# An attention, expert and gated block on one core: the gate row by transposes, output stores issued two units late, the second weights loaded into borrowed tiles

## The chip, the core and the metric

The kernel runs on one core of a Trainium2 chip. The metric is the time of one execution on the device in microseconds, the median of several. A core has TensorE (matmuls; PE in the profile, PEld for its weight loads), VectorE (DVE), ScalarE (ACT), GpSimd (POOL) and SyncE (SP), whose queue here issues nearly all transfers between HBM and the on-chip memory SBUF. Matmuls write into the eight banks of PSUM, from which VectorE or ScalarE must read them before a bank is used again. Each engine works through its own list in order; semaphores order the engines among one another.

## The reference

Three steps follow each other: attention over 32 memory slots a head, a mixture of experts with one expert for each token, and a gated feed-forward layer. Cut to what matters here:

```python
a = softmax(phi); k_m = einsum('bhsm,bhsd->bhmd', a, k); v_m = einsum('bhsm,bhsd->bhmd', a, v)
x = softmax(q @ k_m.T / 8) @ v_m                  # 8 batches, 8 heads, 576 positions, 64 wide
logits = x @ w_gate + modality_bias[modality_id]  # 4608 tokens, 8 experts
e_idx = argmax(logits); gate_w = softmax(logits)[e_idx]
out[mask_e] = gate_w * (relu(x @ w1[e]) @ w2[e])  # 512 -> 1024 -> 512
out = (sigmoid(out @ w_gate2) * (out @ w_val)) @ w_out   # 512 -> 1536 -> 512
```

The code for experts other than the first stands behind a test at run time and is not entered in the profiled execution.

## The kernel before

All matmuls with 288 or more columns run in three terms: each float32 operand is cut into a high and a low part (`split`: a ScalarE cast, then a VectorE subtraction), and high times high, high times low and low times high are added in PSUM (`gemm`, L383 to L385).

**Prologue** (to about 45 us). Batch 0 gets its phi softmax, transposes, pooled keys and values (`pool_kv`, `keep_kv`), scores and the first weights folded with the pooled values (`fold`, which needs all of `w1s`). The second expert weights `w2` come in four parts of 512 KB, first as they are into a tile `late`, then split into `w2h` and `w2l`. `late` has the tag `kv`: it uses the same memory as the keys and values of batch 0. `warm` issues matmuls whose results nobody reads.

**Expert stage** (45 to about 530 us), one pass for each batch of 576 tokens. An `Expert` has 32 units: for each half of 288 tokens eight `hidden` units (six matmuls, evicted by ScalarE into `hh`, then by VectorE into `hl`) and eight half-tiles `y_part` (twelve matmuls; the second of a pair ends with VectorE's product of the PSUM tile and the gate row `gb`, L413, and the store of `yt` to the DRAM tensor `x2d`, L420). `side(i)` puts the preparation of later batches beside the units, at numbered slots: `scores`, `normalize`, `attn_transpose`, `gate_logits` and `gating` of the next batch, `phi_softmax`, `phi_transpose`, `pool_kv`, `keep_kv` and `gate_cols` (L248) of the one after, and two `fold` steps at slots 28 and 30, each of whose two PSUM banks are evicted by `split` (L116, L117). PSUM is shared out by tags: four banks `mm`, two `tr`, one `sc`, one `kv`.

**The gate row.** `gating` leaves a gate weight for each token in `gt`, 128 partitions by 5 columns. The expert needs it along the free axis on every partition. `gate_store` (L353) writes `gt` to a DRAM row `gd` in pieces of 4 bytes, `gate_rows` (L357) loads that row into all partitions as `gb`. Both stand on SyncE's queue, and the load waits until the store has landed.

**Rounding.** `Narrow` takes the weights of the third step, which come as 8-byte numbers, to float32: `load` brings 512 KB into one of two buffers `raw` (L437), `round` begins with a ScalarE step (L444), goes on with five on VectorE and one on GpSimd into one of two buffers `f`, and ends with a store to the DRAM tensor `wd` (L451). There are 36 of them, spread over the slots of the batches.

**Order.** The prologue keeps its written order (`in_order`). Elsewhere a scheduler orders each engine's list, so that roundings, for instance, end before batch 5.

**Gated stage** (from about 535 us). It reads `x2d` and `wd` in five blocks of tokens; its `Quad` and `Out` functions are the same before and after.

Of the kernel before, what the change touches and what calls it, by code (L numbers as in the profile page):

```python
# [18 lines left out]
P = 128  # L19
B, H, S, DH, M = 8, 8, 576, 64, 32  # L20
D = 512
# [20 lines left out]
def attn_moe_glu_kernel(ctx: ExitStack, tc: tile.TileContext, qT, phiT, kvp, mod, wg, mbias, w1, w2, wgv, out):  # L42
# [6 lines left out]

    x2d = dram.tile([P, NP, N], F32, name="x2d")  # L50
    wd = dram.tile([NC2, P, F2], F32, name="wd")
    gd = [dram.tile([1, NT * P], F32, name=f"gd{i}") for i in range(2)]
    sd = dram.tile([NC2, P, 4, 256], F32, name="sd")

    def ps_one(tag):
# [95 lines left out]
    class Att:  # L151
# [197 lines left out]
        def gating(self, bias=None, sel=None):  # L349
            run(self.gating_steps(bias, sel))  # L350

        def gate_store(self):
            nc.sync.dma_start(gd[self.odd].rearrange("o (t p) -> (o p) t", p=P), self.gt)  # L353

        def gate_rows(self):
            self.gb = ap.tile([P, S], F32, name="gb", bufs=2)
            nc.sync.dma_start(self.gb, gd[self.odd][:, :S].to_broadcast([P, S]))  # L357

    def fold(x, n, tags=("mm", "mm"), later=False):
        if x.first is not None and n == 0:  # L360
# [18 lines left out]
    def gemm(pm, steps, lo, hi):  # L379
        n = len(steps)  # L380
        for i in range(lo, hi):
# [2 lines left out]
            T.matmul(pm, wh, xl, start=False, stop=False)  # L384
            T.matmul(pm, wl, xh, start=False, stop=i == n - 1)  # L385

    class Expert:
        def __init__(self, a, add=False):
            self.a = a
# [2 lines left out]
        def hidden(self, half, fc):  # L392
            a = self.a
            if fc == 0:
                self.hh = ap.tile([P, F1 // P, HS], F32R, name="hh")
                self.hl = ap.tile([P, F1 // P, HS], F32R, name="hl")
            pm = ps_one("mm")[:, :HS]
            f = slice(fc * P, (fc + 1) * P)
            s = slice(half * HS, (half + 1) * HS)
            gemm(pm, [(a.vmh[:, g, f], a.vml[:, g, f], a.ahT[:, g, s], a.alT[:, g, s]) for g in range(2)], 0, 2)  # L400
            A.activation(self.hh[:, fc, :], pm, AF.Relu)  # L401
            V.scalar_tensor_tensor(out=self.hl[:, fc, :], in0=pm, scalar=0.0, in1=self.hh[:, fc, :].bitcast(F32), op0=ALU.max, op1=ALU.subtract)  # L402

        def y_part(self, half, dc, part):
            if part == 0:
                self.pm = ps_one("mm")[:, :HS]
            pm = self.pm
            d = slice(dc * P, (dc + 1) * P)
            steps = [(w2h[:, fc, d], w2l[:, fc, d], self.hh[:, fc, :], self.hl[:, fc, :]) for fc in range(F1 // P)]
            gemm(pm, steps, 4 * part, 4 * part + 4)  # L410
            if part == 1:
                yt = ap.tile([P, HS], F32, name="yt", bufs=2)
                V.tensor_tensor(out=yt, in0=pm, in1=self.a.gb[:, half * HS : (half + 1) * HS], op=ALU.mult)  # L413
                c0 = self.a.at_b * S + half * HS
                dst = x2d[:, dc, ds(c0, HS)]
                if self.add:
                    old = ap.tile([P, HS], F32, name="yold", tag="gt_old")
                    nc.sync.dma_start(old, dst)
                    V.tensor_tensor(out=yt, in0=yt, in1=old, op=ALU.add)
                nc.sync.dma_start(dst, yt)  # L420

        def units(self):
            u = []
# [5 lines left out]
    class Narrow:  # L429
# [9 lines left out]
        def round(self):  # L439
            top = self.raw[:, :, 1]  # L440
            nxt = self.raw.bitcast(U16)[:, :, 1]
            f = ap.tile([P, D], F32, name="f", bufs=2)
            fi, tf = f.bitcast(I32), self.raw.bitcast(F32)[:, :, 1]
            A.activation(f, tf, AF.Abs, scale=2.0**16)  # L444
            V.tensor_scalar(f, f, 2.0, None, op0=ALU.max)
            V.tensor_scalar(top, top, -0x80000000, None, op0=ALU.bitwise_and)
            V.scalar_tensor_tensor(out=fi, in0=fi, scalar=3, in1=top, op0=ALU.logical_shift_left, op1=ALU.bitwise_or)
            V.tensor_scalar(top, fi, -0x800000, None, op0=ALU.bitwise_and)
            V.scalar_tensor_tensor(out=tf, in0=nxt, scalar=2.0**-36, in1=tf, op0=ALU.mult, op1=ALU.mult)
            G.tensor_tensor(out=f, in0=f, in1=tf, op=ALU.add)  # L450
            nc.sync.dma_start(wd[self.c, :, self.lo : self.lo + D], f)  # L451

    routed = {}

# [11 lines left out]
    def other_experts(vm):  # L466
# [6 lines left out]
        with tc.For_i(1, E, 1) as e:  # L473
# [3 lines left out]
            with tc.If(mine > 0):  # L477
# [7 lines left out]
                with tc.For_i(0, B // 2, 1) as pair:  # L485
                    two = [Att(b, pair) for b in range(2)]
                    for a in two:
                        a.load_phi()
                        a.load_kv()
                        a.phi_softmax()  # L490
                        pool_batch(a)
                        a.vmh, a.vml = vm[a.b]
                    for a in two:
                        for n in range(2):
                            fold(a, n)
                    for a in two:
                        a.load_q()
                        for t in (0, 2, 4):
                            a.scores(t)
                            a.normalize(t)  # L500
                            a.attn_transpose(t)
                            a.gate_logits(t)
                        bias = ap.tile([P, NT, E], F32, name="bias1")
                        nc.sync.dma_start(bias, biasd[:, ds(a.at_b * NT, NT), :])
                        a.gating(bias, sel)
                        a.gate_store()
                        a.gate_rows()
                        run(Expert(a, add=True).units())

# [4 lines left out]
    def side(i):  # L514
        u = {}

        def at(slot, f, *args):
            u.setdefault(slot, []).append((f, *args))
# [16 lines left out]
        if i + 1 < B:  # L535
# [21 lines left out]
            at(15 + lag, c.attn_transpose, 4)  # L557
            at(16 + lag, c.gate_logits, 4)
            at(16 + lag, c.gating)
            at(21 if i else 28, c.gate_store)  # L560
            at(26 if i else 31, c.gate_rows)
            for n in range(2):
                at(28 + 2 * n, fold, c, n)
        if i + 2 < B:
# [1 line left out]
        if i == 0:  # L566
            at(0, b0.gate_logits, 0)
            at(1, b0.gate_logits, 2)
            at(1, b0.attn_transpose, 4)
            at(2, b0.gate_logits, 4)  # L570
            at(2, w2_parts[3].split)
            at(4, b0.gating)
            at(6, b0.gate_store)
            at(8, b0.gate_rows)
            at(6, bat[2].load_kv)
            at(8, in_order, start)
        lo = max(0, 5 * i - 2)
        for k, n in enumerate(range(lo, min(5 * i + 3, NK))):
            w = Narrow(n)
            slot = 6 * k if i else 11 + 6 * k  # L580
            at(slot, w.load)
            at(slot + 4, w.round)
        return u

    bat = [Att(b) for b in range(B)]
# [2 lines left out]
    b0.load_phi()  # L588
    b0.load_kv()
    nc.scalar.dma_start(wgt, wg)  # L590
    late = sp.tile([P, 9, D], F32, name="late", tag="kv")
    for k, part in enumerate(w2_parts):
        part.load(w2[0], late[:, 2 * k : 2 * k + 2, :])
    b0.load_q()
    for part in w1_parts:
        part.load(w1[0])

    def in_order(start):
        last = {}
# [18 lines left out]

    warm(WARM[0])
    b0.phi_softmax()  # L620
    for g in range(2):
        b0.phi_transpose([g])
        b0.phi_transpose([g], True)
        warm(WARM[1] if g == 0 else 0)
        b0.pool_kv(g)
    b0.scale_kv()
    w2_parts[0].high()
    b0.keep_kv()
    w2_parts[0].low(V)
    for part in w2_parts[1:3]:  # L630
        part.split()
    warm(WARM[2])
    b0.scores(0)
    b0.scores(2)
# [193 lines left out]
    for i in range(B):  # L828
# [16 lines left out]
        for unit in ex.units():  # L845
            run([unit])
            run(u.get(s, []))
            s += 1

    with tc.If(routed["rest"] > 0):  # L850
        vm = first["vm"]
        other_experts(((vm["vmh0"], vm["vml0"]), (vm["vmh1"], vm["vml1"])))
# [155 lines left out]
```

## Time and profile before

| | |
|---|---|
| median of 3 runs | 1361.11 us (1360.92 to 1365.38) |
| profiled execution, its own time | 1364.61 us |
| its span | 1362.5 us |
| PE, PEld busy | 1287.9 us (95%), 1146.7 us (84%) |
| DVE, ACT, POOL busy | 802.7, 568.8, 86.7 us |
| mean granted TensorE clock | 0.963 of full speed |
| bytes moved | 176.32 MB, mean 129 GB/s |

The profile is of one execution. Its rows give times from the span's start; a wait is an engine's idle time just before an instruction, with what ended it. A granted clock of 1.00 is 2.4 GHz and 0.50 is 1.2 GHz, the two levels.

### The profile page before, as it was taken

Reading aid. Unit: us, or ns where it says so; the run is one execution under the profiler, and the core shown is the slowest. Engines: PE = TensorE matmul, PEld = TensorE weight load, DVE = VectorE, ACT = ScalarE, POOL = GpSimd, SP = SyncE. Lnnn points to the kernel's source line nnn. Section 1 sums busy time; section 2 is a strip of 40 time slices with the busy share of each in tenths; the row PEclk is TensorE's granted clock in tenths of the full one; section 3 lists DMA queues with packets and bytes.
Section 4 is the critical chain, followed back from the end, with each engine's and each line's share of the span. In section 5 each row is a group of like instructions: output and inputs, shape, how many; then the busy total and the mean of one; then the engine's idle time right before and its main releaser. Section 6 shows DMA issues by size and latency. Waiting matters only on the chain.

```text
span 1362.5 us, 20067 instructions
## 1 busy us (share of the span) xinstructions
PE 1287.9 (95%) x7810; PEld 1146.7 (84%) x7810; DVE 802.7 (59%) x1591; ACT 568.8 (42%) x1109; POOL 86.7 (6%) x92
## 2 busy tenths in 40 slices
PE   5879879796999998999999999999999999999998
PEld 5778859695998998998889988899889988788787
DVE  1746658584944643878446684566646675465532
ACT  2333323241423322556345563456435563455422
POOL 2202212121200000000000000000000000000000
PEclk7789889897999998999999999999999999999999
DMA  8567576767632111434243343434342342432212
GB/s 310 159 155 170 188 162 213 163 219 140 219 73 82 64 40 65 145 124 147 70 152 124 130 130 93 146 124 136 97 155 93 124 142 83 139 123 94 62 39 85
DMA packets 74886, 176.32 MB, mean 129 GB/s; under 512 B 12320, under 2 KB 21024, under 8 KB 71712
## 3 DMA queue, kind: packets, MB, share of 16 engines
q1 hardware_dynamic: 73776, 173.85, 41.3%
q8 instruction: 63, 1.03, 0.3%
q10 hardware_dynamic: 1008, 1.11, 0.2%
q14 instruction: 39, 0.32, 0.1%
HBM read 140.31 MB, written 34.62 MB: 128 GB/s over the span
## 4 chain that ended last, share of the span: by engine, by line
PE 55%; DMA 3%; DVE 2%; ACT 0%; issue 0%; DVEq 0%; SPq 0%
PE pstr L743 20%; PE pskv L743 10%; PE pssc L743 5%; PE psmm L887 4%; PE psmm L886 4%; PE psmm L885 4%; PE pstr L887 1%; PE pstr L886 1%; PE pstr L885 1%; DMA out_dram<-ot 1%; DMA xq<-x2d 1%; PE pssc L887 1%; PE pskv L887 1%; PE pssc L886 1%; PE pskv L886 1%; PE pssc L885 1%
## 5 line engine op out<-in xcount | busy, mean ns | idle before, releaser
L743 PE MATMUL pstr<-xcvml,aw 128*128 128x448 f32 (+1 forms) x720 | 160.7, 370 | 2.2 <-DVE gw2h L755 2.0
L383 PE MATMUL psmm<-hh,w2h 128*128 128x288 f32 x512 | 159.2, 311 | 0.8 <-issue 0.8
L384 PE MATMUL psmm<-hl,w2h 128*128 128x288 f32 x512 | 153.5, 300 | 2.5 <-DVE hl L402 2.5
L385 PE MATMUL psmm<-hh,w2l 128*128 128x288 f32 x512 | 153.4, 300 | 0.3 <-issue 0.3
L743 PEld LDWEIGHTS pstr<-xcvml,aw 128*128 128x128 f32 x720 | 133.5, 188 | 20.2 <-DVE gw2h L755 5.5
L383 PEld LDWEIGHTS psmm<-hh,w2h 128*128 128x128 f32 x512 | 98.5, 192 | 16.6 <-issue 15.9
L384 PEld LDWEIGHTS psmm<-hl,w2h 128*128 128x128 f32 x512 | 98.7, 193 | 2.7 <-DVE hl L402 2.7
L117 DVE TENSOR_TENSOR aw<-raww,aw 128x512 fp32r<-128x512 f32 x120 | 65.9, 555 | 57.6 <-ACT aw L116 57.1
L385 PEld LDWEIGHTS psmm<-hh,w2l 128*128 128x128 f32 x512 | 98.5, 192 | 0.1
L887 PE MATMUL psmm<-ow,gl 128*128 128x512 f32 x240 | 93.5, 389 | 0.0
L886 PE MATMUL psmm<-ow,gh 128*128 128x512 f32 x240 | 93.4, 389 | 0.0
L885 PE MATMUL psmm<-ow,gh 128*128 128x512 f32 x240 | 93.4, 389 | 0.0
L743 PE MATMUL pstr<-xckv,aw 128*128 128x448 f32 (+1 forms) x360 | 85.7, 372 | 3.9 <-DVEq L850 3.9
L383 PE MATMUL psmm<-ahT,vmh 128*128 128x288 f32 x256 | 81.7, 319 | 7.5 <-DVE hl L402 6.1
L743 PE MATMUL pstr<-xcvmh,aw 128*128 128x448 f32 (+1 forms) x360 | 84.5, 370 | 0.9 <-DVE tex L755 0.8
L743 PE MATMUL pssc<-xckv,aw 128*128 128x448 f32 (+1 forms) x360 | 85.0, 371 | 0.0
L743 PE MATMUL pskv<-xcvmh,aw 128*128 128x448 f32 (+1 forms) x360 | 84.8, 370 | 0.0
L743 PE MATMUL pskv<-xcxc,aw 128*128 128x448 f32 (+1 forms) x360 | 83.8, 368 | 0.0
L401 ACT ACTIVATE hh<-psmm 128x288 fp32r<-128x288 f32 x128 | 50.8, 410 | 72.2 <-PE psmm L385 71.7
L384 PE MATMUL psmm<-alT,vmh 128*128 128x288 f32 x256 | 79.5, 310 | 0.3 <-DVE alT L117 0.3
L385 PE MATMUL psmm<-ahT,vml 128*128 128x288 f32 x256 | 77.8, 304 | 0.0
L117 DVE TENSOR_TENSOR aw<-sums,aw 128x512 fp32r<-128x512 f32 x120 | 77.6, 684 | 0.0
(221 smaller groups left out, 2623.3 us busy)
## 6 DMA issues: line engine op xcount, KB each, us to landing
raww<-wd SPq DMA_DIRECT2D x60, 512.0 KB, 4.2
sums<-sd SPq DMA_DIRECT2D x48, 512.0 KB, 3.3
raw<-in_wgv_dram SPq DMA_DIRECT2D x36, 512.0 KB, 4.0
oraw<-wd SPq DMA_DIRECT2D x60, 256.0 KB, 2.7
kv<-in_kv_dram SPq DMA_DIRECT2D x9, 1024.0 KB, 13.6
qt<-in_q_dram SPq DMA_DIRECT2D x8, 1152.0 KB, 5.5
wd<-f SPq DMA_DIRECT2D x36, 256.0 KB, 2.4
x2d<-yt SPq DMA_DIRECT2D x64, 144.0 KB, 2.6
```

Of the source, the lines that this page charges most:

```text
L117: lo_engine.tensor_tensor(out=lo, in0=src, in1=hi.bitcast(F32), op=ALU.subtract)
L383: T.matmul(pm, wh, xh, start=i == 0, stop=False)
L384: T.matmul(pm, wh, xl, start=False, stop=False)
L385: T.matmul(pm, wl, xh, start=False, stop=i == n - 1)
L401: A.activation(self.hh[:, fc, :], pm, AF.Relu)
L743: T.matmul(o, wk, xk, start=start and k + a == 0, stop=k == KH - 1 and a == 2, skip_group_check=not start)
L885: T.matmul(o, gh, w[:, 0], start=c == 0, stop=False)
L886: T.matmul(o, gh, w[:, 1], start=False, stop=False)
L887: T.matmul(o, gl, w[:, 0], start=False, stop=c == NC2 - 1)
```

## The change

Four things change. The gate row no longer goes through DRAM: for each of the five columns of `gt`, TensorE transposes the column, repeated over 128 columns, into a bank with tag `tr`, and ScalarE copies the two banks to `gb`. An output tile's store is put on a list and issued by the next but one unit (`send_stores`). The rounded weights' store becomes a step of its own two slots after the rounding, which itself moves from slot +4 to slot +5. And the four second-weight parts are loaded into two tiles with the tags `hh` and `hl`, which the expert's activations use later; two parts before the queries and two behind; their splits move forward among batch 0's steps, the last of them into the prologue.

```diff
-    gd = [dram.tile([1, NT * P], F32, name=f"gd{i}") for i in range(2)]
...
-        def gate_store(self):
-            nc.sync.dma_start(gd[self.odd].rearrange("o (t p) -> (o p) t", p=P), self.gt)
-
         def gate_rows(self):
             self.gb = ap.tile([P, S], F32, name="gb", bufs=2)
-            nc.sync.dma_start(self.gb, gd[self.odd][:, :S].to_broadcast([P, S]))
+            for t in range(NT):
+                rows = P if t < 4 else 64
+                if t in (0, 4):
+                    pg = ps_one("tr")
+                T.transpose(pg[:, (t % 4) * P : (t % 4) * P + rows], self.gt[:rows, t : t + 1].to_broadcast([rows, P]), ident[:rows, :rows])
+                if t == 3:
+                    A.copy(self.gb[:, 0:512], pg)
+            A.copy(self.gb[:, 512:S], pg[:, 0:64])
...
+    stores = []
+
+    def send_stores():
+        while stores:
+            nc.sync.dma_start(*stores.pop())
...
             if fc == 0:
                 self.hh = ap.tile([P, F1 // P, HS], F32R, name="hh")
                 self.hl = ap.tile([P, F1 // P, HS], F32R, name="hl")
+            if fc == 1:
+                send_stores()
...
             if part == 1:
+                send_stores()
                 yt = ap.tile([P, HS], F32, name="yt", bufs=2)
...
-                nc.sync.dma_start(dst, yt)
+                stores.append((dst, yt))
...
             G.tensor_tensor(out=f, in0=f, in1=tf, op=ALU.add)
-            nc.sync.dma_start(wd[self.c, :, self.lo : self.lo + D], f)
+            self.f = f
+
+        def store(self):
+            nc.sync.dma_start(wd[self.c, :, self.lo : self.lo + D], self.f)
...
-            at(21 if i else 28, c.gate_store)
-            at(26 if i else 31, c.gate_rows)
+            at(22 if i else 29, c.gate_rows)
...
-            at(2, w2_parts[3].split)
             at(4, b0.gating)
-            at(6, b0.gate_store)
-            at(8, b0.gate_rows)
+            at(7, b0.gate_rows)
...
-            at(slot + 4, w.round)
+            at(slot + 5, w.round)
+            at(slot + 7, w.store)
...
-    late = sp.tile([P, 9, D], F32, name="late", tag="kv")
-    for k, part in enumerate(w2_parts):
-        part.load(w2[0], late[:, 2 * k : 2 * k + 2, :])
+    spare = [ap.tile([P, 4, D], F32, name="late", tag=tag) for tag in ("hh", "hl")]
+    late = [t[:, k : k + 2, :] for t in spare for k in (0, 2)]
+    for part, raw in zip(w2_parts[:2], late):
+        part.load(w2[0], raw)
     b0.load_q()
+    for part, raw in zip(w2_parts[2:], late[2:]):
+        part.load(w2[0], raw)
...
-    for g in range(2):
-        b0.phi_transpose([g])
-        b0.phi_transpose([g], True)
-        warm(WARM[1] if g == 0 else 0)
-        b0.pool_kv(g)
+    b0.phi_transpose([0])
+    b0.phi_transpose([0], True)
+    warm(WARM[1])
+    b0.pool_kv(0)
+    w2_parts[0].high()
+    b0.phi_transpose([1])
+    b0.phi_transpose([1], True)
+    b0.pool_kv(1)
+    w2_parts[0].low(V)
+    w2_parts[1].high()
+    w2_parts[1].low(V)
     b0.scale_kv()
-    w2_parts[0].high()
+    w2_parts[2].high()
     b0.keep_kv()
-    w2_parts[0].low(V)
-    for part in w2_parts[1:3]:
-        part.split()
+    w2_parts[2].low(V)
+    w2_parts[3].split()
...
+    send_stores()
     with tc.If(routed["rest"] > 0):
```

Three places show how instructions move. The first is SyncE's queue in the prologue, from the second piece of batch 0's keys and values on; `late` are the second weights, `qt` the queries, `w1s` the first weights, `raw` two loads for the rounding. Before:

```order
L182 DMA kv<-in_kv_dram 128x2048
L437 DMA raw<-in_wgv_dram 128x1024 x2
L134 DMA late<-in_moe_w_dram 128x1024 x4
L188 DMA qt<-in_q_dram 128x2304
L124 DMA w1s<-in_moe_w_dram 128x2x512 x4
```

After:

```order
L181 DMA kv<-in_kv_dram 128x2048
L133 DMA late<-in_moe_w_dram 128x1024 x2
L187 DMA qt<-in_q_dram 128x2304
L133 DMA late<-in_moe_w_dram 128x1024 x2
L123 DMA w1s<-in_moe_w_dram 128x2x512 x4
```

The raw loads are gone from here (they follow later), and the queries stand between the second weights' halves.

The second is SyncE's queue in batch 1, from the keys and values of a later batch on, up to the rounding loads beside the two folds; `gd` and `gb` are the gate store and load, `wd` rounded weights, `x2d` output tiles, `raw` loads for the rounding. Before:

```order
L182 DMA kv<-in_kv_dram 128x2048
L353 DMA gd_65<-gt 128x5x1
L451 DMA wd<-f 128x512
L420 DMA x2d<-yt 128x288
L451 DMA wd<-f 128x512
L357 DMA gb<-gd_65 128x576
L437 DMA raw<-in_wgv_dram 128x1024
L420 DMA x2d<-yt 128x288
L437 DMA raw<-in_wgv_dram 128x1024
```

After:

```order
L181 DMA kv<-in_kv_dram 128x2048
L468 DMA wd<-f 128x512 x2
L394 DMA x2d<-yt 128x288
L451 DMA raw<-in_wgv_dram 128x1024 x2
L394 DMA x2d<-yt 128x288 x2
L468 DMA wd<-f 128x512
L451 DMA raw<-in_wgv_dram 128x1024
```

The gate store and load are gone, and the two raw loads stand together behind the first output store of the second half.

The third is TensorE at the end of the hidden units of batch 1's second half, where the gate columns of batch 3 stand (L248 before, L247 after; `vp` holds the pooled values). Before:

```order
L383 MATMUL psmm<-ahT,vmh_1091 128x288
L384 MATMUL psmm<-alT,vmh_1091 128x288
L385 MATMUL psmm<-ahT,vml_1092 128x288
L383 MATMUL psmm<-hh,w2h 128x288
L248 MATMUL pskv<-wgt,vp_105 64x8 x4
L384 MATMUL psmm<-hl,w2h 128x288
```

After:

```order
L388 MATMUL psmm<-ahT,vml_1086 128x288
L357 MATMUL pstr<-ident,gt 128x128 x4
L386 MATMUL psmm<-ahT,vmh_1085 128x288
L387 MATMUL psmm<-alT,vmh_1085 128x288
L388 MATMUL psmm<-ahT,vml_1086 128x288
L357 MATMUL pstr<-ident,gt 128x64
L386 MATMUL psmm<-ahT,vmh_1085 128x288
L387 MATMUL psmm<-alT,vmh_1085 128x288
L388 MATMUL psmm<-ahT,vml_1086 128x288
L247 MATMUL pskv<-wgt,vp_103 64x8 x4
```

Four transposes of the gate column now stand ahead of the last hidden unit, the fifth, into the second bank, behind half of it, and the gate columns behind them all.

## Rows read from the trace of the kernel before

**Rows 1.** Waits of PE from 60 to 430 us: total us, times, longest.

```profile
PE psmm L369 <- DVE vml L117: 27.8, 3, 10.6
PE pskv L248 <- ACT vp L242: 7.3, 4, 6.0
```

**Rows 2.** Windows by batch: busy us (x instructions), clock, DMA share, GB/s.

```profile
45.00:131.00 86.00, 73.90 (x626) 66.70 (x627) 55.23 (x150) 30.50 (x76) 16.53 (x12) 0.86 0.64 147
131.00:205.00 74.00, 58.80 (x493) 53.90 (x492) 44.35 (x113) 21.21 (x48) 13.11 (x10) 0.86 0.66 188
205.00:270.00 65.00, 56.20 (x496) 51.25 (x494) 44.06 (x113) 20.55 (x49) 14.08 (x11) 0.92 0.68 186
270.00:337.00 67.00, 55.96 (x489) 51.02 (x488) 43.41 (x111) 20.15 (x48) 14.06 (x11) 0.90 0.72 180
337.00:391.00 54.00, 53.52 (x492) 49.89 (x492) 38.81 (x95) 18.54 (x44) 11.24 (x9) 1.00 0.63 191
```

**Rows 3.** Timeline of SyncE's queue, batch 1: start us, us, what.

```profile
174.10 0.61 SPq L353 DMA_DIRECT2D gd<-gt  x1
...
190.94 0.32 SPq L357 DMA_DIRECT2D gb<-gd  x1
191.32 0.43 SPq L437 DMA_DIRECT2D raw<-in_wgv_dram  x1
```

**Rows 4.** Timeline of ScalarE, batch 1; in brackets idle before and its releaser.

```profile
197.38 0.66 ACT L444 ACTIVATE f<-raw 128x512 f32<-128x512 f32 x1 [15.58 <-DMA raw<-in_wgv_dram]
197.95 1.05 ACT L116 CAST vmh<-psmm 128x512 fp32r<-128x512 f32 x2
```

**Rows 5.** Timeline of VectorE, batch 1.

```profile
198.08 0.43 DVE L445 TENSOR_SCALAR f<-f 128x512 f32<-128x512 f32 x1 [12.95 <-ACT f L444]
```

**Rows 6.** Timeline of PE, batch 1.

```profile
186.15 1.09 PE L369 MATMUL psmm<-w1s,vp 64*32 64x512 f32 x16
...
199.49 2.55 PE L369 MATMUL psmm<-w1s,vp 64*32 64x512 f32 x16 [8.88 <-DVE vml L117]
```

**Rows 7.** Landing of the gate stores of line 353.

```profile
DMA to landing us min/median/max: 16.8/17.7/18.6
```

**Rows 8.** DMA issues: engine, count, KB each, median us to landing.

```profile
raw<-in_wgv_dram SPq DMA_DIRECT2D x36, 512.0 KB, 4.0
```

**Rows 9.** Waits of SyncE's queue: total us, times, longest.

```profile
SPq L357 <- DMA gd<-gt: 65.4, 8, 11.0
```

**Rows 10.** Waits of all engines.

```profile
ACT f L444 <- DMA raw<-in_wgv_dram: 97.4, 21, 20.7
```

**Rows 11.** Timeline of VectorE, batch 0.

```profile
85.16 0.82 DVE L413 TENSOR_TENSOR yt<-psmm,gb 128x288 f32<-128x288 f32 x2 [10.28 <-DMA gb<-gd]
```

**Rows 12.** Timeline of SyncE's queue, batch 4.

```profile
386.40 0.32 SPq L357 DMA_DIRECT2D gb<-gd  x1
386.82 20.76 SPq L420 DMA_DIRECT2D x2d<-yt  x5
```

**Rows 13.** Timeline of SyncE's queue, prologue.

```profile
16.28 1.75 SPq L134 DMA_DIRECT2D late<-in_moe_w_dram  x4
18.08 0.59 SPq L188 DMA_DIRECT2D qt<-in_q_dram  x1
```

**Rows 14.** Timeline of PE, prologue.

```profile
17.80 0.83 PE L617 MATMUL psmm<-ident 128*128 128x128 f32 x6
...
27.31 7.06 PE L263 MATMUL psmm<-kmb,qt 128*128 128x64 f32 x32 [8.68 <-DMA qt<-in_q_dram]
...
45.64 0.40 PE L383 MATMUL psmm<-ahT,vmh 128*128 128x288 f32 x1 [0.34 <-ACT ahT L116]
```

**Rows 15.** Timeline of PE, four transposes.

```profile
71.39 0.60 PE L210 MATMUL pstr<-ident,pht 128*128 128x128 f32 x4
```

**Rows 16.** Line 211, a copy of 512 columns: ns min/median/max.

```profile
L211 ACT COPY at<-pstr x16: 581/586/592, 8.5 to 417.5; 128x512 f32<-128x512 f32 x16
```

**Rows 17.** GB/s in 40 equal slices of the first 45 us.

```profile
GB/s 0 53 120 136 327 447 424 414 410 401 415 404 62 15 0 98 240 408 386 408 427 421 426 364 402 395 390 394 411 459 400 430 422 381 137 0 0 15 0 0
```

More of the change, by code (lines that the diff above doesn't have):

```diff
@@ L419, in y_part @@
                     V.tensor_tensor(out=yt, in0=yt, in1=old, op=ALU.add)
-                nc.sync.dma_start(dst, yt)
+                stores.append((dst, yt))
+                if self.add:
+                    send_stores()
         def units(self):
@@ L505, in other_experts @@
                         a.gating(bias, sel)
-                        a.gate_store()
                         a.gate_rows()
@@ L848, in attn_moe_glu_kernel @@
             s += 1
+    send_stores()
     with tc.If(routed["rest"] > 0):
```

## The prediction

> **What bounds the kernel now.** I read the waits of the engines first, then the timeline of one stall engine by engine, then windows cut by batch. In the expert stage, from 45 to about 530 us, TensorE stood idle longest in front of the weight fold, 27.8 us in three waits of up to 10.6 us, and in front of the gate columns, 7.3 us [rows 1]. The windows put this at batches 0 to 3: they take 86, 74, 65 and 67 us at granted clocks of 0.86 to 0.92, while batch 4, with the same TensorE work and nearly as much VectorE work (38.8 us of it against 44), takes 54 us at clock 1.00 with PE busy for 53.52 of them [rows 2]. So 54 us is what TensorE needs for such a batch when nothing is late, and batches 1 to 3 take 206 us for what would be 162.
>
> One stall shows the cause. SyncE's queue issues the gate store at 174.10 and the gate load only at 190.94, since that waits for the store to land; the next raw weights stand right behind it, at 191.32 [rows 3]. ScalarE meanwhile stood 15.58 us before the rounding step that needs those raw weights, until 197.38, and the eviction of the fold's banks is the next thing on its queue [rows 4]; VectorE stood 12.95 us behind ScalarE [rows 5]. The second fold, whose banks were not free, began at 199.49 after 8.88 us of idle [rows 6]. It is no accident: the eight gate stores take 16.8 to 18.6 us to land [rows 7] where raw weights take 4.0 [rows 8]; SyncE stood 65.4 us at the eight loads behind them [rows 9], and ScalarE 97.4 us before raw weights [rows 10]. In batch 0 the round trip reached VectorE directly, 10.28 us before the first output tile [rows 11]. Batch 4 has the round trip too, its load at 386.40, but no raw load is left behind it, only output stores [rows 12], and it runs freely. That is the control.
>
> Before the stage, the second weights wait until 16.28 us for the tile that the first keys and values still hold, and the queries stand behind them, at 18.08 [rows 13]. TensorE waits 8.68 us for the queries, its 32 score matmuls then take 7.06 us, and the first expert matmul runs at 45.64 [rows 14].
>
> **The gate row by transposes.** Eight stores and eight loads go, with the wait between them. Added for each batch are five transposes and two ScalarE copies. Four such transposes take 0.60 us in a row [rows 15], the fifth adds about 0.15; so 0.75 us of TensorE for each batch, 6 us in all. The copies, 0.59 us for 512 columns [rows 16] and less for 64, lie beside TensorE work, ScalarE being busy 21 of 74 us in batch 1 [rows 2]; without that cover they would add under 1 us a batch. Queued behind the transposes on TensorE are the last hidden unit, the gate columns and the output tiles. Two things can be late there: the gate values, which come out of some sixteen short VectorE steps after the logits, and the second of the two banks, which the key and value copies must leave first. Gate columns already wait for those copies at almost this place. From below the wait is nothing, as in batch 4; from above it is the longest one at the gate columns, 6.0 us [rows 1], which came while VectorE stood at the gate load. With that load gone I take 0.5 us a batch.
>
> TensorE: Matmul & The Clock Gate, of the Trainium skill (Part 4: PE-mode transpose), has about 275 ns for a 128x128 transpose inside a kernel. In the trace they overlap, four in 0.60 us; if each cost its whole 275 ns, forty would be an estimated 11 us instead of 6.
>
> **The stores.** An output store now enters SyncE's queue two units after its tile, and a rounded weight's store two slots after its rounding, so that neither should hold the queue for long. By itself a wait of SyncE costs nothing; it matters where raw weights stand behind. In the new order of batch 1 two raw loads still stand behind the first output store of the second half. From that tile's end it is three issues of about 0.4 us [rows 3] and 4.0 to land [rows 8], some 5.2, and 0.7 for each rounding step on ScalarE [rows 4]. TensorE ends the first fold three half-tiles later: two took the 3.4 us between the fold's end, 187.24, and the idle's beginning, 190.61, and the fold 1.09 [rows 6], so some 6.2 us. The first eviction is thus about in time or a microsecond late, VectorE's two roundings may push the second fold by one or two more, and the next batch's first hidden tiles can meet the third raw load. Bounds: nothing, as in batch 4, and 8.88 us as now. I take 3 us for each of batches 1 to 3, nearer the lower end, since the long landing that made the upper one is gone.
>
> **Batches 1 to 3:** 206 - 3 x (54 + 0.75 + 0.5 + 3) = 31 us gained; bounds 42 (no wait left) and 18 (over half of the excess stays).
>
> **Batch 0** takes 86 us. Against batch 4 it also pools batch 1's keys and values, which I put at 5 us of TensorE, makes two gate rows, 1.5, and starts at the lower clock, 5, and I leave it 5 for TensorE's waits for gate values and activations: 54 + 16.5 = 70.5, a gain of 15. Bounds: 8, little more than the 6.0 us wait at the gate columns, and 20.
>
> **The prologue.** The first four weight parts no longer wait for a tile, and the two raw loads move behind the prologue. By the tiles' sizes 0.6 MB of phi, 2.4 of keys and values and 1.0 of weights lie ahead of the queries' 1.2: 5.2 MB. The row of transfer rates has 0.35 MB moved by 4.5 us and then some 0.41 MB a microsecond [rows 17], so they land near 16.3 us. The keys' chain ends near 18, where the warm-up matmuls stand now [rows 14], so scores can start there, 9 us sooner. All first weights make 8.3 MB and land near 24 us against a fold that now begins when the scores end, 34.4: 9 or 10 us. The weight splits that move ahead on ScalarE and VectorE could hold the keys' chain for some 3 us; scores at the higher clock could return as much. I take 9 us; bounds 4 and 13. The activation tiles that the weights borrow are free when GpSimd has split the last part, which stands ahead of the first hidden tile by the whole score and fold chain.
>
> **Batches 4 to 6** only lose, 0.75 for transposes and up to 0.5 for their wait: -3 us. The gated stage keeps its instructions.
>
> **Sum:** 31 + 15 + 9 - 3 = 52 us. The profiled execution took 1364.61 us, 3.5 above the median of 1361.11; 1364.6 - 52 = 1312.6, and 1309 against the median. The bounds sum to 42 + 20 + 13 - 2 = 73 and 18 + 8 + 4 - 6 = 24, so 1288 to 1337.
>
> **Rivals.**
> *The queue stays late behind stores* (0.13). SyncE's order still puts raw loads behind output stores and rounded stores; if those are late themselves, ScalarE still stops at the rounding. For it: SyncE waits in more places than the gate. Against it: batch 4's first half has rounds and stores, and PE idled under half a microsecond in all of it [rows 2]. Batches 1 to 3 then gain only 12, batch 0 gains 8, the start 9, less 3: 26 us, 1335.
> A rule of the Trainium skill points the same way: DMA: Bandwidth & Descriptors (Anatomy of one DMA) fits 2.0 us plus the bytes over 436 GB/s, by which the 2.5 KB store would land in an estimated 2 us and taking it away free little. The trace disagrees, with 16.8 us at least [rows 7]; the same page (Rules for kernel authors) has a non-contiguous last dimension lowered to one descriptor for each element, which the store's 4-byte pieces are.
> *The wait moves to TensorE* (0.04). Until now only SyncE waited for the gate value; now TensorE does, in order. If VectorE is held as long as in [rows 5], 12.95 us, when the gate value is due in each of the five batches with rounding, TensorE loses 65 us against the 52 gained: 1374. It decides for slower from 12 us a batch on.
> *The start gains nothing* (0.08): the moved splits hold the keys' chain, or the first weights land no sooner. 1318.
> My forecast has 0.75; alone it would reach from 1292 to 1326.
>
> A measurement of this kernel tells about 0.5%, 7 us, from no change. All cases but the second rival are faster by more, and the first one's worst end comes near it: 0.94 faster, 0.02 within, 0.04 slower. The range, 1288 to 1335, leaves out the second rival and the far half of the first.
>
> **What would show it.** Right: no gate store or load on SyncE; ScalarE's wait before raw weights far below 97 us; no fold wait over 4 us; batches 1 to 3 at 56 to 60 us; scores from near 18 us and the first expert matmul near 36; a gate row's transposes within a microsecond. Wrong: TensorE idle before the transposes of the gate column or the gate columns for several microseconds a batch; VectorE waiting for output stores to land; raw weights still late, then behind output or rounded stores; scores as late as now.

## The result and the profile after

The changed kernel takes 1313.09 us (median of 4 runs, 1312.05 to 1317.84) where the kernel before takes 1362.78 beside it (4 runs, 1360.92 to 1365.38): a ratio of 0.9641, 95% interval 0.961 to 0.9672. The forecast was 1309 in a range from 1288 to 1335. A second set of runs, further down, gave 1312.96 and a ratio of 0.9653 (0.964 to 0.9666). The profiled execution took 1317.84 us, the longest of its four; its span is 1315.7.

The page: busy time of the engines, and the granted clock in 40 slices.

```profile
PE 1281.0 (97%) x7850; PEld 1141.7 (87%) x7850; DVE 809.3 (62%) x1593; ACT 574.3 (44%) x1125; POOL 79.4 (6%) x90
...
PEclk9899999999999989999999999999999999999999
```

TensorE is busy for 1281.0 us instead of 1287.9, and 97% of a span that is 46.8 us shorter. So most of what went is idle time. Busy time fell too, although forty transposes were added, since fewer matmuls ran at the lower clock.

Windows by batch of the changed kernel, batches 0 to 6, with the columns of [rows 2]:

```profile
36.00:105.00 69.00, 65.90 (x623) 59.86 (x622) 51.91 (x145) 29.38 (x74) 11.65 (x10) 0.95 0.61 214
105.00:164.00 59.00, 56.59 (x498) 52.21 (x496) 44.56 (x113) 21.85 (x50) 14.17 (x11) 0.97 0.59 195
164.00:226.00 62.00, 56.94 (x497) 52.13 (x495) 50.49 (x119) 21.65 (x52) 16.28 (x13) 0.97 0.64 212
226.00:282.00 56.00, 54.48 (x495) 50.57 (x495) 47.10 (x117) 21.76 (x52) 15.31 (x12) 1.00 0.66 222
282.00:338.00 56.00, 54.11 (x493) 50.30 (x494) 33.85 (x85) 17.75 (x44) 6.65 (x6) 1.00 0.42 141
338.00:392.00 54.00, 54.00 (x499) 50.50 (x498) 26.89 (x73) 16.58 (x41) 2.71 (x3) 1.00 0.15 55
392.00:445.00 53.00, 51.46 (x402) 48.64 (x401) 30.89 (x79) 16.55 (x38) 2.71 (x3) 0.97 0.15 49
```

Batches 0 to 3 take 69, 59, 62 and 56 us where they took 86, 74, 65 and 67, at clocks of 0.95 to 1.00 instead of 0.86 to 0.92. That is 246 us instead of 292; by the columns, 35 of the 46 us are TensorE's idle time (47.1 before, 12.1 after) and 11 its busy time.

The busy time shows that a stall costs more than its own length. The sixteen matmuls of the fold took 1.09 us ahead of the stall of batch 1 and 2.55 us behind its 8.88 us of idle [rows 6]. The window of the kernel before around the second fold has a granted clock of 0.50, the lower level:

```profile
199.40:202.10 2.70, 2.61 (x17) 0.53 (x17) 2.70 (x8) 0.28 (x1) 0.00 (x0) 0.50 0.16 55
```

TensorE's waits from 47 to 445 us (total, times, longest), which answer to [rows 1]:

```profile
PE psmm L386 <- DVE vml L116: 4.0, 4, 1.2
PE pskv L302 <- ACT ahT L115: 2.8, 3, 1.5
PE pstr L357 <- ACT vp L241: 2.5, 2, 1.7
...
PE pstr L357 <- ACT gb L359: 0.7, 1, 0.7
PE pstr L357 <- DVE gt L310: 0.7, 1, 0.7
```

The fold's 27.8 us are gone: no fold is in the list. The transposes of the gate column (L357) wait four times, 3.9 us together, 1.7 at the longest.

Batch 1 again, the place of [rows 3 to 6]. SyncE's queue:

```profile
143.82 5.68 SPq L468 DMA_DIRECT2D wd<-f  x2
151.63 0.34 SPq L394 DMA_DIRECT2D x2d<-yt  x1
152.02 0.92 SPq L451 DMA_DIRECT2D raw<-in_wgv_dram  x2
```

ScalarE in the same stretch, with its idle time in brackets:

```profile
156.22 0.69 ACT L458 ACTIVATE f<-raw 128x512 f32<-128x512 f32 x1 [5.85 <-DMA raw<-in_wgv_dram]
157.47 0.69 ACT L458 ACTIVATE f<-raw 128x512 f32<-128x512 f32 x1 [0.56 <-DMA raw<-in_wgv_dram]
158.05 1.07 ACT L115 CAST vmh<-psmm 128x512 fp32r<-128x512 f32 x2
```

And TensorE, the two folds of the batch and the first hidden unit of the next that waits:

```profile
155.79 1.09 PE L372 MATMUL psmm<-w1s,vp 64*32 64x512 f32 x16
...
160.19 1.39 PE L372 MATMUL psmm<-w1s,vp 64*32 64x512 f32 x16
...
165.30 0.40 PE L386 MATMUL psmm<-ahT,vmh 128*128 128x288 f32 x1 [1.14 <-DVE vml L116]
```

The two raw loads go out behind one output store, at 152.02, and ScalarE waits 5.85 us for the first instead of 15.58. The first fold's banks are evicted from 158.05 on, and the second fold starts at 160.19 without a wait. What is left is 1.14 us at the next batch's hidden units, for VectorE's half of the second eviction. VectorE reached that at 164.56, right behind rounding steps:

```profile
163.96 0.69 DVE L463 SCALAR_TENSOR_TENSOR raw<-raw 128x512 f32<-128x512 uint16 x1
164.56 1.28 DVE L116 TENSOR_TENSOR vml<-psmm,vmh 128x512 fp32r<-128x512 f32 x2
```

In the prologue, which answers to [rows 13, 14], SyncE's queue and then TensorE:

```profile
2.60 3.41 SPq L133 DMA_DIRECT2D late<-in_moe_w_dram  x2
6.06 0.43 SPq L187 DMA_DIRECT2D qt<-in_q_dram  x1
```

```profile
18.45 2.77 PE L635 MATMUL psmm<-ident 128*128 128x128 f32 x12
21.02 3.79 PE L262 MATMUL psmm<-kmb,qt 128*128 128x64 f32 x32
...
34.53 0.40 PE L386 MATMUL psmm<-ahT,vmh 128*128 128x288 f32 x1 [0.34 <-ACT ahT L115]
```

The queries are issued at 6.06 instead of 18.08, and the scores no longer wait for them. The score matmuls take 3.79 us instead of 7.06.

Cut from ScalarE's first hidden eviction of a batch to that of the next, the profiled executions of all kernels stand like this (us; "rest" is batch 7 and the gated stage):

| kernel | start | batch 0 | 1 to 3 | 4 to 6 | rest | span |
|---|---|---|---|---|---|---|
| before | 47.4 | 83.9 | 206.0 | 156.5 | 868.7 | 1362.5 |
| changed | 36.3 | 69.1 | 176.9 | 162.5 | 871.0 | 1315.7 |
| changed, again | 36.5 | 69.1 | 174.1 | 159.3 | 869.8 | 1308.7 |
| 1 gate row only | 46.8 | 76.4 | 172.3 | 159.6 | 870.2 | 1325.3 |
| 2 stores only | 45.9 | 93.1 | 190.2 | 157.2 | 867.4 | 1353.8 |
| 3 start only | 36.6 | 88.9 | 192.8 | 164.3 | 868.0 | 1350.5 |
| 4 gate row undone | 36.3 | 81.5 | 201.2 | 160.1 | 869.3 | 1348.3 |
| 5 unread trip, 4-byte pieces | 36.3 | 89.7 | 193.3 | 158.7 | 870.1 | 1348.1 |
| 6 unread trip, 20-byte pieces | 36.5 | 70.6 | 177.8 | 159.4 | 868.5 | 1312.9 |
| 7 transposes twice | 36.4 | 70.4 | 182.0 | 160.7 | 867.6 | 1317.2 |
| 8 gate row later | 36.4 | 68.9 | 171.6 | 159.3 | 869.9 | 1306.1 |
| 9 no store change | 36.5 | 68.9 | 176.2 | 159.4 | 869.1 | 1310.1 |
| 10 no store change, gate row later | 36.4 | 70.3 | 174.1 | 159.8 | 869.3 | 1309.9 |

### The profile page after: what moved, and what is told of

The parts are those of the page before. It is cut to its first block, busy times and chain, and to the rows that moved or that the text cites. A ratio compares the mean times of both kernels' runs of the same rounds, so it can differ in the third digit from the quotient of the medians.

```text
span 1315.7 us, 20134 instructions
## 1 busy us (share of the span) xinstructions
PE 1281.0 (97%) x7850; PEld 1141.7 (87%) x7850; DVE 809.3 (62%) x1593; ACT 574.3 (44%) x1125; POOL 79.4 (6%) x90
## 4 chain that ended last, share of the span: by engine, by line
PE 57%; DMA 3%; DVE 2%; ACT 0%; issue 0%; DVEq 0%; SPq 0%
PE pstr L766 21%; PE pskv L766 10%; PE pssc L766 5%; PE psmm L911 4%; PE psmm L910 4%; PE psmm L909 4%; DMA xq<-x2d 2%; PE pstr L910 1%; PE pstr L911 1%; PE pstr L909 1%; PE pssc L910 1%; PE pssc L911 1%; PE pskv L910 1%; PE pskv L911 1%; PE pssc L909 1%; PE pskv L909 1%
## 5 line engine op out<-in xcount | busy, mean ns | idle before, releaser
L386 PEld LDWEIGHTS psmm<-hh,w2h 128*128 128x128 f32 x512 | 97.5, 190 | 13.2 <-issue 12.5
L766 PE MATMUL pskv<-xcxc,aw 128*128 128x448 f32 (+1 forms) x360 | 83.9, 368 | 0.0
L766 PEld LDWEIGHTS pstr<-xckv,aw 128*128 128x128 f32 x360 | 68.2, 190 | 11.0 <-issue 4.1
```

The source lines that it names most:

```text
L386: T.matmul(pm, wh, xh, start=i == 0, stop=False)
L766: T.matmul(o, wk, xk, start=start and k + a == 0, stop=k == KH - 1 and a == 2, skip_group_check=not start)
```

## The experiments

The theory: SyncE's queue stood still behind a load that waited for the landing of the gate store, and raw weights behind it came late. The rivals: the output and rounded stores held the queue; or the gate row's own arrival was what counted.

**The three parts, each alone, and the gate row taken back.** Experiment 1 is the kernel before with only the gate row's part of the change:

```diff
-            nc.sync.dma_start(self.gb, gd[self.odd][:, :S].to_broadcast([P, S]))
+                T.transpose(pg[:, (t % 4) * P : (t % 4) * P + rows], self.gt[:rows, t : t + 1].to_broadcast([rows, P]), ident[:rows, :rows])
...
-            at(21 if i else 28, c.gate_store)
-            at(26 if i else 31, c.gate_rows)
+            at(22 if i else 29, c.gate_rows)
```

> The kernel before with only the gate row made by transposes; stores, rounding slots and the start as before. Theory (the gate row's round trip through DRAM on SyncE's queue held the raw weights, and ScalarE, VectorE and TensorE behind them): batches 0 to 3 lose most of their excess, about 15 and 29 us, transposes cost up to 6, so some 1325 us against 1363, and ScalarE's wait before raw weights falls from 97 us to under 75. Rival (output and rounding stores hold the queue just as much): 1350 or more, with ScalarE still stopped for 10 us or more in front of a fold's eviction.

Measured: 1327.34 us against 1360.1, ratio 0.9774 (0.9745 to 0.9803), a gain of 33. TensorE's waits in its expert stage:

```profile
PE pstr L357 <- DVE gt L310: 4.1, 1, 4.1
PE psmm L386 <- DVE vml L116: 3.6, 3, 1.3
```

No fold waits, with the stores where they were. ScalarE's wait before raw weights is 73.6 us, under the 75 expected. Experiment 2 is the kernel before with only the store part:

```diff
-                nc.sync.dma_start(dst, yt)
+                stores.append((dst, yt))
...
-            at(slot + 4, w.round)
+            at(slot + 5, w.round)
+            at(slot + 7, w.store)
```

> The kernel before with only the output stores two units later, the rounded stores as a step of their own and the rounding a slot later. Theory (gate round trip): within 7 us of 1363, since the load behind the gate store still holds the queue for some 17 us a batch. Rival (the stores): 1335 or less, and fold waits of 8 us gone.

Measured: 1357.46 us, ratio 0.9987 (0.9974 to 1.0001): no difference that can be told. TensorE still waits for the fold's banks:

```profile
PE psmm L369 <- DVE vml L117: 17.7, 3, 6.8
PE psmm L383 <- DVE vml L117: 6.8, 3, 5.8
```

The rival that blames the stores falls. Experiment 3 is the kernel before with only the new start:

```diff
-    late = sp.tile([P, 9, D], F32, name="late", tag="kv")
+    spare = [ap.tile([P, 4, D], F32, name="late", tag=tag) for tag in ("hh", "hl")]
```

> The kernel before with only the second weights loaded into the activation tiles and their splits moved forward. If the start adds up with the rest, the first expert matmul comes 9 to 11 us sooner and the whole is 9 to 11 us shorter, about 1352. Rival: the stage behind absorbs the start, since the raw loads of the rounding now stand behind the prologue: 1360 to 1365 although the first matmul is early.

Measured: 1352.7 us, ratio 0.9946 (0.993 to 0.9963), a gain of 7.4, although the first hidden eviction comes 10.8 us earlier. The table does not show where the rest went: batch 0 takes 5 us more and batches 4 to 6 take 7.8 more than before, but batches 1 to 3 take 13.2 less, and the two profiled executions differ by 12.0. The fold now waits five times:

```profile
PE psmm L369 <- DVE vml L117: 36.6, 5, 7.8
```

Experiment 4 is the changed kernel with the gate row sent through DRAM again:

```diff
-            at(22 if i else 29, c.gate_rows)
+            at(21 if i else 28, c.gate_store)
+            at(26 if i else 31, c.gate_rows)
```

> The changed kernel with the gate row sent through DRAM again; stores and start stay changed. Theory (gate round trip): 1345 to 1355, the start's gain alone is left, with fold waits of 5 to 10 us back. Rival (the stores did it): 1313 to 1322, the round trip being hidden once nothing else holds the queue.

Measured: 1350.31 us, ratio 0.9931 (0.9914 to 0.9947). The waits are back, on TensorE and on SyncE:

```profile
PE psmm L369 <- DVE vml L117: 13.3, 3, 6.1
```

```profile
SPq L357 <- DMA gd<-gt: 51.1, 7, 10.3
```

So the gate row is worth 33 us from the side of the kernel before, and some 38 from the side of the changed one (0.9931 - 0.9653 of 1361).

**The queue or the gate row's arrival.** Experiment 5 keeps the transposes and adds the old store, and a load of eight of its values into a tile that nobody reads:

```diff
+        def idle_store(self):
+            nc.sync.dma_start(gd[self.odd].rearrange("o (t p) -> (o p) t", p=P), self.gt)
+
+        def idle_load(self):
+            idle = ap.tile([P, 8], F32, name="idle", bufs=2)
+            nc.sync.dma_start(idle, gd[self.odd][:, :8].to_broadcast([P, 8]))
...
+            at(21 if i else 28, c.idle_store)
             at(22 if i else 29, c.gate_rows)
+            at(26 if i else 31, c.idle_load)
```

> The changed kernel, and beside the transposes the old gate store and, five slots later, a load of its first 8 values into a tile that nobody reads. Nothing depends on that load; it only stands on SyncE's queue until the store has landed. Theory (the queue's head is what costs): 1340 to 1352, the gain of the gate row all but gone, with ScalarE waiting 10 to 20 us for raw weights before folds. Rival (what cost was that VectorE needed the gate row late, or bandwidth of the small pieces): within 5 us of 1313.

Measured: 1349.9 us against 1361.19, ratio 0.9911 (0.9882 to 0.994). Nothing computed depends on the load, and some 35 of the change's 47 to 49 us (by its two ratios) are gone (0.9911 - 0.9653 of 1361). SyncE's queue in batch 1, from the unread store on:

```profile
159.88 0.38 SPq L353 DMA_DIRECT2D gd<-gt  x1
...
175.10 0.32 SPq L357 DMA_DIRECT2D idle<-gd  x1
175.47 0.42 SPq L459 DMA_DIRECT2D raw<-in_wgv_dram  x1
```

The raw load stands right behind the unread one. ScalarE waits for it, with the fold's bank next on its list, and TensorE's second fold comes late:

```profile
181.07 0.66 ACT L466 ACTIVATE f<-raw 128x512 f32<-128x512 f32 x1 [13.04 <-DMA raw<-in_wgv_dram]
181.63 1.06 ACT L116 CAST vmh<-psmm 128x512 fp32r<-128x512 f32 x2
```

```profile
183.91 2.55 PE L380 MATMUL psmm<-w1s,vp 64*32 64x512 f32 x16 [6.00 <-DVE vml L117]
```

In batch 1 this is the chain of [rows 3 to 6], step for step, with a load that serves nothing.

Elsewhere in this run the scattered store itself does it. At the end of batch 0 a raw load goes out right behind the unread store, 17 us ahead of the unread load. SyncE's queue, then ScalarE:

```profile
102.86 0.37 SPq L353 DMA_DIRECT2D gd<-gt  x1
103.28 0.52 SPq L459 DMA_DIRECT2D raw<-in_wgv_dram  x1
...
120.14 0.35 SPq L357 DMA_DIRECT2D idle<-gd  x1
```

```profile
116.62 0.66 ACT L466 ACTIVATE f<-raw 128x512 f32<-128x512 f32 x1 [9.07 <-DMA raw<-in_wgv_dram]
```

That raw load lands after 13.2 us, where the median of its line is 4.6, and it stands behind no load that waits. The same holds for ScalarE's waits of 9.00 us to 243.53 and 12.30 us to 308.38: their raw loads go out at 232.26 and 293.05, behind the scattered store and ahead of the unread load. So three of the five longest waits in this run are raw loads that travel beside the scattered store, and two (11.68 us to 73.89, 13.04 us to 181.07) stand behind the unread load. The expectation had put the small pieces' effect on other transfers among the rivals that leave the time at 1313; since experiment 5 has these pieces too, it does not exclude it.

Experiment 6 differs from it in one thing: the unread store writes the five values of a partition side by side, 128 pieces of 20 bytes instead of 640 of 4.

```diff
-            nc.sync.dma_start(gd[self.odd].rearrange("o (t p) -> (o p) t", p=P), self.gt)
+            nc.sync.dma_start(gd[self.odd].rearrange("o (p t) -> (o p) t", p=P), self.gt)
```

> As the run before, but the unused store writes the five values of a partition side by side, 128 pieces of 20 bytes instead of 640 of 4. Theory (the long landing of scattered pieces): the store lands in 2 to 6 us, the load holds the queue that much shorter, and the time is within 8 us of 1313. Rival (any round trip on the queue costs the same): 1340 to 1352 again.

Measured: 1314.96 us, ratio 0.9657 (0.963 to 0.9684), as fast as without the trip. The stores' landing in experiment 5, and in experiment 6:

```profile
DMA to landing us min/median/max: 8.8/14.8/15.4
```

```profile
DMA to landing us min/median/max: 1.4/2.3/8.6
```

So neither the extra transfers nor their place in the queue cost the time, but the long landing of the scattered store. It costs in two ways: the load that waits for it holds the queue (SyncE stands 56.3 us at the unread loads in experiment 5 and 11.6 in experiment 6), and raw loads beside it land late. How the cost divides between the two is open, since the scattered store was not run without the load. In the kernel before, it is the first way: the raw loads before ScalarE's three longest waits (15.58, 18.31 and 20.71 us) go out at 191.32 [rows 3], 255.83 and 322.74, each right behind a gate load.

DMA: Bandwidth & Descriptors, of the Trainium skill (Anatomy of one DMA — SWDGE (gpsimd) path), fits 2.0 us plus the bytes over 436 GB/s, measured on transfers that GpSimd issues; the prediction applied it to SyncE's store without saying so. On SyncE's queue here the 2.3 us of the 20-byte pieces lie close to it, the 14.8 us of the same 2.5 KB in 4-byte pieces do not.

**What the transposes cost, and where they stand.** Experiment 7 writes each transpose of the gate column twice into the same place, 40 more in all:

```diff
+                for _ in range(2):
+                    T.transpose(pg[:, (t % 4) * P : (t % 4) * P + rows], self.gt[:rows, t : t + 1].to_broadcast([rows, P]), ident[:rows, :rows])
```

> The changed kernel with each transpose of the gate column issued twice, into the same place: 40 more. The prediction's 0.15 us each makes 6 us, 1319. If they lie in slack of TensorE: under 2 us. If each costs its whole 0.27 us: 11 us, 1324.

Measured: 1318.49 us, ratio 0.9672 (0.9642 to 0.9702). Against the changed kernel's two ratios that is 0.0019 to 0.0031 of 1361 us, 3 to 4 us, or 5 by the medians; the intervals overlap, so it is a size and no more. Each record of a transpose is long, as the changed kernel's line 357 shows (ns, min/median/max):

```profile
L357 PE MATMUL pstr<-ident,gt x40: 266/272/323, 49.2 to 428.4; 128*128 128x128 f32 x32, 64*128 64x64 f32 x8
```

TensorE: Matmul & The Clock Gate, of the Trainium skill (Part 4: PE-mode transpose), has about 275 ns, close to the 272 of these records. Four in a row (at 144.70 in batch 1) take 0.60 us in this kernel too, since their records overlap:

```profile
144.70 0.60 PE L357 MATMUL pstr<-ident,gt 128*128 128x128 f32 x4
```

By 272 each the forty would have cost 11 us.

Experiment 8 moves the changed kernel's transposes from slots 22 and 29 to 25 and 31:

```diff
-            at(22 if i else 29, c.gate_rows)
+            at(25 if i else 31, c.gate_rows)
```

> The changed kernel with the gate row's transposes three slots later, behind the gate columns. If TensorE's waits in front of the transposes and their place among the hidden units cost what the windows suggest, 0.5 to 1.5 us a batch: 1305 to 1310. Rival (those waits are only moved, to the gate columns or the activations): within 3 us of 1313.

Measured: 1310.91 us (1308.24 to 1316.03), ratio 0.9638 (0.9605 to 0.9671). It is the lowest median, but the interval holds the changed kernel's 0.9653.

**Whether the store part earns anything in company.** Experiment 9 is the changed kernel without it:

```diff
-                stores.append((dst, yt))
+                nc.sync.dma_start(dst, yt)
...
-            at(slot + 5, w.round)
-            at(slot + 7, w.store)
+            at(slot + 4, w.round)
```

> The change without its store part: gate row by transposes and the new start, but output tiles and rounded weights stored as before. Theory A (the parts nearly add, the store part is worth its lone 3 us or a little more, since nothing slow stands in the queue any longer): 1316 to 1321 us, ScalarE's longest wait before raw weights well over 6 us in the expert stage, TensorE idle at hidden units. Rival (the late stores are what makes room for raw loads once the gate row is gone): 1325 or more. Second rival (the store part earns nothing beside the others): within 1 us of the changed kernel, 1312 to 1314.

Measured: 1314.03 us, ratio 0.9665 (0.9651 to 0.9678), where the changed kernel, beside it, has 1312.96 and 0.9653 (0.964 to 0.9666). My theory of 1316 to 1321 fell: the second rival was right, and the store part earns about 1 us, which its interval does not tell from nothing.

Experiment 10 is experiment 9 with the gate row's slots of experiment 8, and the last run is the changed kernel itself:

> As the version without the store part, with the gate row's transposes at slots 25 and 31 instead of 22 and 29. If TensorE's waits at the transposes cost something (0.7 to 4 us a batch in the profiles so far), it is 1 to 3 us faster than that version; if they only take the place of other waits, the same.

> The changed kernel itself, in the same call as the two versions without the store part, so that they stand against the same runs of the kernel before: 1311 to 1316 us, ratio 0.964.

Measured: 1314.02 us, ratio 0.9667 (0.9653 to 0.9681), the same as experiment 9; and 1312.96 for the changed kernel. Where the transposes stand in these slots makes no difference that can be told, so experiment 8's 2 us stay unproved, and no version was found that beats the changed kernel beyond its interval.

## Why the prediction was right

**The cause.** It named SyncE's queue behind the gate load, with raw weights behind it, and the kernel before shows that path at its three longest waits. Experiments 1 and 4 show that the round trip costs the time, and 5 and 6 that its scattered pieces do: the gain goes with an unread trip in 4-byte pieces, and stays with one in 20-byte pieces. The path was not isolated from the second way, raw loads that land late beside the store, which the prediction did not have. The gate values' own arrival was not it: even batch 0, where VectorE had waited for them [rows 11], takes 89.7 us with the unread trip, though its gate row comes by transposes.

**Batches 1 to 3** were to gain 31 us and gained 29.1 in the first profile, 31.9 in the second (206.0 - 174.1). The 3 us of stall kept for each batch were the right size: with 54 for the matmuls and 1.25 for the transposes and their wait, 174.1 leaves 2.8 a batch and 176.9 leaves 3.7. Part of it is where the prediction put it, at the second eviction and the next hidden tiles, 1.1 to 1.2 us each time. In batch 1 VectorE's roundings hold it; in batches 2 and 3 the third raw load, which the prediction named, is behind it as well. ScalarE waited for that load 5.03 us to 224.61 and 5.12 us to 280.67, and VectorE idled 1.27 and 1.36 us for ScalarE just ahead of the eviction, in batch 2:

```profile
225.31 0.45 DVE L459 TENSOR_SCALAR f<-f 128x512 f32<-128x512 f32 x1 [1.27 <-ACT f L458]
```

ScalarE's wait before raw weights fell less than I wrote: 68.5 us instead of 97.4. Its pieces are short, 5.9 instead of 20.7, and but for those two places hidden:

```profile
ACT f L458 <- DMA raw<-in_wgv_dram: 68.5, 28, 5.9
```

The 62 us of batch 2 lie above the 56 to 60 forecast. There the second transpose bank came 1.7 us late, and the two windows around it show the engines ahead of it full (VectorE 3.86 and ScalarE 3.96 of 4 us) and then a granted clock of 0.62:

```profile
204.00:208.00 4.00, 2.32 (x22) 1.85 (x20) 3.86 (x13) 3.96 (x14) 1.01 (x1) 1.00 0.97 403
208.00:212.00 4.00, 4.00 (x22) 4.00 (x21) 2.86 (x6) 0.15 (x2) 1.34 (x2) 0.62 0.68 201
```

**Batch 0** was to gain 15 and gained 14.8. Experiment 1 splits it: with the gate row alone it takes 76.4 us, so half of the gain needs the earlier start as well. No run isolates how; by the traces, about half of the 7.3 us is a wait for the gate value before the transposes (4.1 us in experiment 1, 0.7 in the changed kernel) and about half TensorE's busy time (69.4 us at clock 0.91, 66.0 at 0.95). That the sum came out is partly luck, since its three terms of 5 us did not measure 5: the window has 3.1 us of idle; the clock, 0.95 over 69 us, makes some 7 us at half speed, a loss of 3.4; and what is left of the busy time beside the 54 and the two gate rows, some 7 us, is the pooling.

**The start** was to gain 9 and gained 11.1. Scores came at 21.02, not near 18, behind twelve warm-up matmuls; the sum had left these out, and that it gave 2 us too few is the clock. From the first score matmul to the first expert matmul took 18.34 us at clock 0.67 before, and 13.53 at 1.00 after. The windows of the kernel before, and of the changed one:

```profile
27.30:45.64 18.34, 17.99 (x128) 14.51 (x128) 7.91 (x16) 3.55 (x7) 2.24 (x3) 0.67 0.69 259
```

```profile
21.00:34.53 13.53, 13.19 (x130) 10.52 (x128) 8.07 (x17) 4.57 (x8) 4.45 (x3) 1.00 0.83 320
```

The prediction had named a return of the clock, as large as the splits' 3 us, and set the two off against each other. The stretch gave 4.8, and the earlier scores 6.3 (27.31 - 21.02).

**Batches 4 to 6** were to lose 3 and lost 6.0 in the first profile, 2.8 in the second. Over all eight batches the transposes' 6 us came out at 3 to 5, not clear of the intervals, and their wait, 0.5 a batch or 4 for eight, at 3.9, all of it in batches 0 to 2.

**The sum.** The terms make 52 from the profiled 1364.6. The spans differ by 46.8 in the first profile of the changed kernel and by 53.8 in the second, the medians by 49.7 and 47.8. So no term of the sum failed, and the 4 us between 1309 and 1313 are less than what two executions of the changed kernel differ by. Three of its signs missed by a little: the scores at 21.02, the 62 us of batch 2, and the second transpose bank, 1.7 us late instead of within a microsecond. The rest of the program, batch 7 and the gated stage, scatters between 867.4 and 871.0 over all kernels, whatever was changed.

**The store part** was costed at nothing by itself, and experiments 2 and 9 bear that out with 2.6 and 1 us, neither beyond its interval. The parts alone give 33, 2.6 and 7.4, 43 together, and the whole gives 48 to 50. It is the start that is worth more in company: experiments 9 and 1 differ in it alone and stand 0.0109 of 1361 us apart, some 15 (0.9774 - 0.9665), against 7.4 alone. The table puts this in batch 0, which takes 5.0 us more with the start alone and 7.5 less where the start joins the gate row. That the held queue swallows an earlier start is argued from this and not shown: in batches 1 to 3 the start alone gained 13.2, and the three parts' profiled spans alone add up to 57.9 (37.2, 8.7 and 12.0), more than the whole.

**The rivals.** The wait did not move to TensorE: the gate value itself cost it 0.7 us in one place (4.1 in experiment 1, in batch 0). The queue is not late behind stores in a way that costs: SyncE stands longer at output stores than before, 168.9 us against 148.4, and no fold waits. SyncE's waits of the kernel before, and of the changed one:

```profile
SPq L420 <- DVE yt L413: 148.4, 36, 10.8
```

```profile
SPq L394 <- DVE yt L425: 168.9, 43, 11.9
```

## What to carry to other kernels

A load that waits for an earlier transfer's landing stops every transfer behind it on its queue; look at what stands there before blaming the load's own reader. Time such a trip by the landing of its pieces in the trace, not by its bytes, and look at what else lands late beside it. And count more than the idle time of a stall: here the matmuls behind it ran at the lower clock.

## What the hardware showed that was not expected

The same 2.5 KB from the same tile land in 14.8 us (median) as 640 pieces of 4 bytes and in 2.3 us as 128 pieces of 20 bytes; worked out from the two, an estimate of some 24 ns for each piece more ((14.8 - 2.3) us over 512; 30 by the 17.7 us of [rows 7]). A raw load of 512 KB that went out 0.4 us behind such a store landed after 13.2 us, against a median of 4.6; in experiment 6, behind the 20-byte pieces, the one at the same place (94.22) took 5.2.

Short stretches at the lower clock come and go between executions of one kernel. Batches 1 and 6 of the changed kernel took 58.9 and 52.4 us in the first profile, with 3.4 us at the lower clock in each, and 56.2 and 49.2 in the second, with none: 5.9 us of the 7.0 between the two spans. Half speed for 3.4 us loses 1.7, so about 3.4 of the 5.9 are the clock; the rest is shorter waits, such as the 1.5 us before the gate logits (L302) in batch 6, which the second profile does not have.
